# Two groups of second-stage products moved ahead of a mixing and of a transpose step, in a convolution and spectral mixing kernel

## The chip, the cores and the metric

The kernel runs on one core of one Trainium2 chip. The metric is the device time of one execution in microseconds (us): the median of several runs. A profiled execution gives, beside it, a trace of every instruction, and its span (the time from the first to the last recorded instruction).

## The reference

The input `x` has 8 sequences (B) of 3264 steps (S) with 192 channels (D). Two stages follow each other.

```python
# 1. a causal convolution over 7 steps, with softmax weights for each of 8 heads (24 channels each)
w = softmax(weight)                                  # (8 heads, 7 taps)
x = einsum('hk,bskhg->bshg', w, x_unf)               # x_unf: the last 7 steps, zero padded
# 2. a mixing of the 64 lowest Fourier modes, and a product with a matrix and a relu
X = rfft(x, axis=1)[:, :64]                          # Xr, Xi
Yr = einsum('bmd,mde->bme', Xr, w_r) - einsum('bmd,mde->bme', Xi, w_i)
Yi = einsum('bmd,mde->bme', Xr, w_i) + einsum('bmd,mde->bme', Xi, w_r)
y = irfft(Y, n=S, axis=1)                            # Y is zero above mode 64
u = x + y
return u + maximum(u @ w_ch, 0)
```

## The kernel before, in words

The order of the instructions on each engine is written out by hand (a manual schedule); each engine works through its own list in that order, and semaphores hold an instruction until what it needs is there. The two halves of a pair of sequences are always worked on together, so there are four pairs, q = 0 to 3.

**Convolution and transform (to about 71 us).** TensorE (PE) convolves tiles of 128 steps with a banded matrix (L297), VectorE (DVE) and ScalarE (ACT) copy the results to `xall`, and products with a table of sines and cosines (`ftab`, L358) give the Fourier modes of each pair.

**Mixing (to about 98 us).** The 64 modes are mixed in 16 groups of four: `mix(g, bank)` issues twelve small products (L515) with the weights of group g, which the DMA queue of GpSimd (POOL) brings in. There are eleven places for weights; a mixing asks, after its last product, for the weights of group g + 11, if there is such a group. Two groups share a PSUM bank, `zm[0]` or `zm[1]`. `mix_copy` (L525, L527, on ACT) scales the sums into `ymix`, and `mix_trans` transposes `ymix` by two or four products (L398) into the two banks `ze`, from which DVE (L552) and ACT (L554) copy them into `yet`. Between the steps of one mixing, `some(n)` puts other work, the transposes of `xall` into `ct` (L398, evicted at L393 and L395), as long as there is any.

**End of the mixing, where the change lies (about 98 to 105.5 us).** Groups 14 and 15 are mixed each by itself, and other work stands between their steps:

- `zw_pair(q, bw, by)` makes the second-stage products of a later pair, q = 1, 2 or 3. For both halves t of the rows (weights `wm` and `w1`) and both sequences of the pair, `zw_mm` issues two products (L591 and L592) of `yet` with the weights. The four of t = 0 write bank `bw`, the four of t = 1 bank `by`. ACT then copies `bw` (L602), DVE copies `by` (L604) into `zwl`. The products read all columns of `yet`, those of the last groups included; what they give for the last eight modes is overwritten later by `late_rows` (L533 to L539), which makes these rows anew and writes them by DMA.
- `both(n, first, "c")` issues the first pieces (six products, L582) of the output pair n of tiles, into the banks `place[n]`. `place[0]` is `sl[0:2]`; `place[1]` are the two banks that `ze` named until then, and from there on `ze` names `sl[2:4]`.
- At the end, four `zw_mm` make the second-stage products of pair 0, and three copies (L690, L691, L692) evict them into `zw`.

**Last stage (from 105.45 us).** For the 104 output tiles, PE adds the remaining products into a ring of eight banks (L716, L647), ACT applies the relu (L640), DVE adds `xall` (L629), and the queue of SyncE (SP) stores the result (L635).

Of the kernel before, what the change touches and what calls it, by code (L numbers as in the profile page):

```python
# [20 lines left out]
def kernel(  # L21
# [107 lines left out]
    def open_psum(side, widths):  # L129

        if side in stacks:
            stacks.pop(side).close()
        es = ExitStack()
        n = npool[0]
        npool[0] += 1
        p = es.enter_context(tc.tile_pool(name=f"ps{n}", bufs=1, space=PSUM, side=side, reuse_waits="tile"))
        stacks[side] = es
        return [p.tile([P, w, 512], F32, tag=f"z{n}_{i}", name=f"z{n}_{i}") for i, w in enumerate(widths)]
# [337 lines left out]
    ze, zm = [z[:, 0, :] for z in z4[0:2]], [z[:, 0, :] for z in z4[2:4]]  # L476
# [33 lines left out]
    def mix(g, bank):  # L510
        yp = bank[:, D * (g % 2):D * (g % 2) + D]
        for j in range(3):
            for p4 in range(4):
                m = 4 * g + p4
                nc.tensor.matmul(yp[32 * p4:32 * p4 + 2 * B, :], xt[:, j, :, m],  # L515
                                 wts[g][:, p4, j, :], start=(j == 0), stop=(j == 2),
                                 tile_position=(0, 32 * p4), skip_group_check=True)
        load_w(g + NW + NL)

    def mix_copy(d, bank, g0, n):  # L520

        g = 2 * d + g0
        srcv = bank[:, D * g0:D * (g0 + n)].rearrange("p (g d) -> p g d", g=n)
        if g == 0:
            nc.scalar.activation(out=ymix[:, 0, :], in_=srcv[:, 0, :], func=ACT.Copy, scale=ascale[:, 0:1])  # L525
            g, n, srcv = 1, n - 1, srcv[:, 1:n, :]
        nc.scalar.activation(out=ymix[:, g:g + n, :], in_=srcv, func=ACT.Copy, scale=2.0 / S)  # L527
# [14 lines left out]
    def mix_trans(d, g0, n):  # L542
        et = [z.bitcast(BF16)[:, 0:n * P].rearrange("p (g k) -> p g k", g=n) for z in ze]
        for t in range(2):
            for g in range(n):
                trans(et[t][:, g, :], ymix[:, 2 * d + g0 + g, 64 * t:64 * t + P])
        m0 = 8 * d + 4 * g0
        for t in range(2):
            dst = yet[:, t, 2 * B * m0:2 * B * (m0 + 4 * n)].rearrange("p (m k) -> p m k", k=2 * B)
            srcv = et[t].rearrange("p g (q k) -> p (g q) k", q=4)[:, :, 0:2 * B]  # L550
            if t == 0:
                nc.vector.tensor_copy(out=dst, in_=srcv)  # L552
            else:
                nc.scalar.copy(out=dst, in_=srcv)  # L554
# [14 lines left out]
    def both(n, first, which, begin=False, end=False):  # L569
        duo, banks = duos[n], place[n]  # L570
        lists = (z_pieces(duo[first], 0, which), z_pieces(duo[1 - first], 1, which))
        old = held.get(n)
        if old is not None and old[0] != first:
            turn(old[1])
        last = [None, None]
        for k in range(max(len(lists[0]), len(lists[1]))):
            for row in range(2):
                lst, bank = lists[row], first ^ row
                if k >= len(lst):
                    continue  # L580
                cols, l, r = lst[k]
                mm = nc.tensor.matmul(target(banks[bank], cols, r), l, r, start=(begin and k == 0),  # L582
                                      stop=(end and k == len(lst) - 1), skip_group_check=True)
                last[row] = mm.ins.name
        held[n] = (first, last)

    def zw_mm(b, o, t):

        cols = slice(D * t, D * t + D)
        last = 2 * MODES * B - B + b + 1  # L590
        nc.tensor.matmul(o, yet[:, 0, b:last:B], wm[:, cols], start=True, stop=False, skip_group_check=True)  # L591
        nc.tensor.matmul(o, yet[:, 1, b:last:B], w1[:, cols], start=False, stop=True, skip_group_check=True)  # L592

    def zw_pair(q, bw, by):

        for t, bank in enumerate((bw, by)):
            for i in range(2):
                zw_mm(2 * q + i, bank[:, D * i:D * i + D], t)
        for t, bank in enumerate((bw, by)):
            dst, srcv = zwl[:, 2 * q - 2:2 * q, t, :], bank[:, 0:2 * D].rearrange("p (b d) -> p b d", b=2)  # L600
            if t == 0:
                nc.scalar.copy(out=dst, in_=srcv)  # L602
            else:
                nc.vector.tensor_copy(out=dst, in_=srcv)  # L604
# [62 lines left out]
    sl = [z[:, 0, :] for z in open_psum("left", (1, 1, 1, 1))]  # L667
# [2 lines left out]
    mix_trans(d, 0, 2)  # L670
    both(0, 1, "c")
    zw_pair(1, ze[0], ze[1])
    d = ND - 1
    mix(NG - 2, zm[1])
    mix_copy(d, zm[1], 0, 1)
    zw_pair(2, sl[2], sl[3])
    mix_trans(d, 0, 1)
    zw_pair(3, zm[0], sl[2])
    mix(NG - 1, zm[1])
    mix_copy(d, zm[1], 1, 1)  # L680

# [127 lines left out]
```

## Time and profile before

| | |
|---|---|
| median of 3 runs | 173.54 us (173.25 to 173.95) |
| the profiled execution | 173.94 us, its span 172.2 us |
| granted clock of TensorE, mean | 0.988 |
| busy in the span | PE 160.6 (93%), weight loads 133.6 (78%), DVE 128.5 (75%), ACT 113.7 (66%), POOL 51.4 (30%) |
| 99.50 to 102.35 us | PE busy 2.21 of 2.85 us |
| 102.35 to 105.45 us | PE busy 3.01 of 3.10 us |
| weight loads (288 KB each) | about 11 us from issue to landing, the last issued at 90.85 us |
| output stores | 384 KB each, 3.8 us from issue to landing |

PE's matmuls are pipelined: a product of 192 columns shows some 250 ns, but products of one kind start about 80 ns apart, so distances between starts say more than durations. "PEld" are PE's weight loads, which run beside its products. In the chain of work, each step is followed back to what released it, and "issue" is time in which the engine waited for nothing that the profile shows. Profile lines name an instruction by its line of the kernel: L604 is DVE's copy of a second-stage bank, wherever `zw_pair` is called.

### The profile page before, as it was taken

Reading aid. Unit: us, or ns where it says so; the run is one execution under the profiler, and the core shown is the slowest. Engines: PE = TensorE matmul, PEld = TensorE weight load, DVE = VectorE, ACT = ScalarE, POOL = GpSimd, SP = SyncE. Lnnn points to the kernel's source line nnn. Section 1 sums busy time; section 2 is a strip of 40 time slices with the busy share of each in tenths; the row PEclk is TensorE's granted clock in tenths of the full one; section 3 lists DMA queues with packets and bytes.
Section 4 is the critical chain, followed back from the end, with each engine's and each line's share of the span. In section 5 each row is a group of like instructions: output and inputs, shape, how many; then the busy total and the mean of one; then the engine's idle time right before and its main releaser. Section 6 shows DMA issues by size and latency. Waiting matters only on the chain.

```text
span 172.2 us, 6925 instructions
## 1 busy us (share of the span) xinstructions
PE 160.6 (93%) x2897; PEld 133.6 (78%) x2897; DVE 128.5 (75%) x262; ACT 113.7 (66%) x226; POOL 51.4 (30%) x93
## 2 busy tenths in 40 slices
PE   6978999999998999979999989999999999999980
PEld 6974866877867777769999765799899898989840
DVE  4899964736737575567767736799998999999980
ACT  8485864545546366377777644688888888888860
POOL 7997522424323352444441000890000000000000
PEclk9999999999999999999999999999999999999995
DMA  2999999999999999999999940488999999989894
GB/s 31 202 203 203 207 201 203 204 204 202 205 202 205 208 205 207 206 206 206 209 203 206 209 69 4 161 298 321 361 334 350 348 320 339 351 318 358 299 386 170
DMA packets 37151, 40.14 MB, mean 233 GB/s; under 512 B 2464, under 2 KB 37120, under 8 KB 37120
## 3 DMA queue, kind: packets, MB, share of 16 engines
q0 software_dynamic: 22816, 19.62, 71.1%
q1 hardware_dynamic: 14304, 20.09, 31.9%
q8 instruction: 22, 0.36, 0.8%
q14 instruction: 9, 0.07, 0.1%
HBM read 39.10 MB, written 20.05 MB: 344 GB/s over the span
## 4 chain that ended last, share of the span: by engine, by line
PE 79%; DMA 10%; POOL 3%; ACT 2%; issue 1%; DVE 1%; POOLq 0%; ACTq 0%; DVEq 0%
PE z L716 34%; PE z L297 16%; PE z L398 12%; DMA xall<-in_x_dram 10%; PE z L358 10%; PE z L515 3%; POOL xall L153 3%; PE z L591 1%; PE z L647 1%; PE z L375 1%; PE z L592 1%; ACT ftab L393 1%; ACT z L479 1%; ACT shared L527 0%; PE z L582 0%
## 5 line engine op out<-in xcount | busy, mean ns | idle before, releaser
L629 DVE TENSOR_TENSOR arena<-z,xall 128x384 f32<-128x384 f32 (+1 forms) x103 | 56.4, 556 | 3.4 <-PE z L716 1.5
L640 ACT ACTIVATE z<-z 128x384 f32<-128x384 f32 x102 | 48.5, 475 | 12.2 <-PE z L716 2.4
L716 PEld LDWEIGHTS <-ct 64*128 64x128 bf16 x600 | 42.3, 94 | 3.7 <-PE z L647 0.6
L716 PE MATMUL z<-arena,ftab 64*128 64x384 bf16 x308 | 44.9, 322 | 0.0
L297 PE MATMUL z<-xall,shared 64*64 64x336 bf16 (+3 forms) x1024 | 39.0, 294 | 2.1 <-ACT shared L238 1.1
L297 PEld LDWEIGHTS <-shared 64*64 64x64 bf16 x1024 | 33.2, 106 | 8.1 <-issue 4.3
L716 PE MATMUL z<-wsw,ct 64*128 64x192 bf16 x300 | 35.1, 243 | 0.0
L344 DVE CAST xall<-z 128x336 bf16<-128x336 f32 (+1 forms) x48 | 22.9, 482 | 12.0 <-PE z L297 9.7
L716 PEld LDWEIGHTS <-ftab 64*128 64x128 bf16 x396 | 29.7, 93 | 2.7 <-issue 0.5
L342 ACT CAST xall<-z 128x336 bf16<-128x336 f32 (+1 forms) x48 | 20.1, 418 | 15.0 <-PE z L297 11.0
L716 PE MATMUL z<-wm,ct 64*128 64x192 bf16 x200 | 29.9, 243 | 0.0
L716 PE MATMUL z<-w,ct 64*128 64x192 bf16 x100 | 24.3, 243 | 0.0
L395 DVE COPY ct<-z 128x1024 bf16<-128x1024 bf16 x27 | 17.4, 685 | 5.5 <-PE z L398 2.4
L398 PE MATMUL z<-ident,xall 128*128 128x128 bf16 x312 | 19.8, 219 | 0.0
L358 PE MATMUL z<-xall,ftab 128*128 128x384 bf16 (+1 forms) x104 | 18.3, 327 | 0.8 <-DVE xall L336 0.8
L398 PEld LDWEIGHTS <-xall 128*128 128x128 bf16 x312 | 17.8, 98 | 1.0 <-issue 0.2
L153 POOL DMA_DIRECT2D xall<-in_x_dram x16 | 15.0, 944 | 10.3 <-DMA xall<-in_x_dram 9.3
L358 PEld LDWEIGHTS <-ftab 128*128 128x128 bf16 (+1 forms) x104 | 9.6, 98 | 8.1 <-issue 1.3
L716 PE MATMUL z<-mixa,ftab 64*128 64x384 bf16 x88 | 13.6, 323 | 0.0
L393 ACT COPY ct<-z 128x1024 bf16<-128x1024 bf16 x12 | 12.1, 1012 | 2.1 <-PE z L398 1.1
L539 POOL DMA_DIRECT2D arena<-xs x16 | 7.9, 504 | 16.9 <-ACT xs L535 16.9
L276 POOL DMA_DIRECT2D arena<-in_moe_w_r_dram x10 | 6.1, 615 | 9.9 <-ACT xall L342 4.7
(113 smaller groups left out, 154.3 us busy)
## 6 DMA issues: line engine op xcount, KB each, us to landing
out_dram<-arena SPq DMA_DIRECT2D x47, 384.0 KB, 3.8
xall<-in_x_dram POOLq DMA_DIRECT2D x8, 672.0 KB, 16.8
xall<-in_x_dram POOLq DMA_DIRECT2D x8, 480.0 KB, 16.8
arena<-in_moe_w_r_dram POOLq DMA_DIRECT2D x10, 288.0 KB, 11.0
arena<-in_moe_w_i_dram POOLq DMA_DIRECT2D x10, 288.0 KB, 11.3
ct<-in_moe_w_r_dram POOLq DMA_DIRECT2D x6, 288.0 KB, 11.4
ct<-in_moe_w_i_dram POOLq DMA_DIRECT2D x6, 288.0 KB, 11.4
out_dram<-arena SPq DMA_DIRECT2D x4, 288.0 KB, 3.5
```

The source lines that it names most:

```text
L153: nc.gpsimd.dma_start(out=xin[:, s0:s0 + nf, 2 * D * i:2 * D * (i + 1)], in_=src)
L297: yield nc.tensor.matmul(o, band[r, h, int(a != a1), c0:c0 + 64], xin5[r, s1:s1 + n, :, a1, dsl], start=(row == 0 and a1 == 0), stop=(row ...
L342: nc.scalar.copy(out=dst[:, a], in_=srcv)
L344: nc.vector.tensor_copy(out=dst[:, a], in_=srcv)
L358: nc.tensor.matmul(xp, ftab[0:k, t, :], xall[0:k, NT * q + t, :, :], start=(t == t0), stop=(t == t1 - 1), skip_group_check=True)
L393: nc.scalar.copy(out=out, in_=in_)
L395: nc.vector.tensor_copy(out=out, in_=in_)
L398: nc.tensor.matmul(o, in_, ident[:], start=True, stop=True, is_transpose=True)
L539: nc.gpsimd.dma_start(out=zwl[k:k + 1, :, :, :].rearrange("p b t d -> p b (t d)"), in_=ylate[r + 2:r + B, :])
L629: nc.vector.tensor_tensor(out=o[0:pn, :, a, :], in0=srcv, in1=xall[0:pn, s + a, :, :], op=ALU.add)
L640: nc.scalar.activation(out=z, in_=z, func=ACT.Relu)
L716: mm = nc.tensor.matmul(target(bank[k], cols, r), l, r, start=first, stop=last, skip_group_check=True)
```

## The change

Two calls of `zw_pair` move. That of pair 2 goes ahead of mixing 14 and its copy, right behind that of pair 1. That of pair 3 goes ahead of the transposes of mixing 14, which then stand right in front of mixing 15. Nothing else is changed, banks included.

```diff
     both(0, 1, "c")
     zw_pair(1, ze[0], ze[1])
+    zw_pair(2, sl[2], sl[3])
     d = ND - 1
     mix(NG - 2, zm[1])
     mix_copy(d, zm[1], 0, 1)
-    zw_pair(2, sl[2], sl[3])
+    zw_pair(3, zm[0], sl[2])
     mix_trans(d, 0, 1)
-    zw_pair(3, zm[0], sl[2])
     mix(NG - 1, zm[1])
     mix_copy(d, zm[1], 1, 1)
```

In the built program PE's list changes accordingly. On ACT, pair 2's copy (L602) goes ahead of mixing 14's (L527), and pair 3's ahead of the transposes' (L554). On DVE, pair 3's copy (L604) goes ahead of the transposes' (L552). The lists of POOL and SP stay the same. Pair 3's products lose their wait for L552 and L554; their fifth gains one for pair 2's L602, which evicts the bank that it writes. The first two L582 pieces of `both(1, 0, "c")` gain one each, for L552 and L554.

## The prediction

> **What bounds the kernel now.** First the page's chain of work that ended last:
>
> ```profile
> PE 79%; DMA 10%; POOL 3%; ACT 2%; issue 1%; DVE 1%; POOLq 0%; ACTq 0%; DVEq 0%
> ```
>
> TensorE (PE) carries the end for 79%, so a stall of PE is paid in full, if the last stage doesn't absorb it. The diff touches only the stretch between the first later pair's products and the last stage. There I read the chain in order of time, from 99 to 106 us (start, duration, what):
>
> ```profile
> 101.64 0.11 DVE arena L604
> 101.75 0.36 issue
> 102.11 0.19 DVE yet L552
> 102.31 0.05 issue
> 102.35 0.30 PE z L591
> ...
> 103.66 0.02 issue
> 103.68 0.34 ACT shared L527
> 104.02 0.05 issue
> 104.06 0.29 PE z L398 x2
> ```
>
> The chain leaves PE twice. At 101.64 it goes over VectorE (DVE): the eviction L604 of pair 2, then the copy L552 of the transposes into `yet`, which pair 3's products (L591/L592) wait for. At 103.68 it goes over ScalarE (ACT): the copy L527 of mixing 15, which the last transposes wait for. The waits of 98 to 112 us agree (engine, line, waited for: us, times, longest):
>
> ```profile
> PE z L591 <- DVE yet L552: 0.6, 1, 0.6
> PEld L398 <- ACT shared L527: 0.7, 2, 0.4
> ```
>
> DVE's own timeline shows why L552 is late: it stands behind L604.
>
> ```profile
> 100.49 0.56 DVE L604 CAST arena<-z 128x384 bf16<-128x384 f32 x1 [1.12 <-DMA arena<-in_moe_w_r_dram]
> 101.64 0.56 DVE L604 CAST arena<-z 128x384 bf16<-128x384 f32 x1 [0.59 <-PE z L592]
> 102.11 0.18 DVE L552 COPY yet<-z 128x64 bf16<-128x64 bf16 x1
> 103.34 0.56 DVE L604 CAST arena<-z 128x384 bf16<-128x384 f32 x1 [1.05 <-PE z L592]
> ```
>
> **The change, part by part.** Nothing is added or removed: 8 products, 12 mixing products, 2 transposes, 3 ACT and 2 DVE copies change places. None of the moved steps issues a DMA (mixings 14 and 15 ask for no further weights), and the queues of SP and POOL keep their order. Pair 3 no longer waits for `yet`, since the transposes that write it now come later. In exchange the first piece of output pair 1 (L582, into the banks that the transposes used) waits for L552 and L554; in the old order that was satisfied long before.
>
> Start-to-start steps of PE, from the timeline: product to product in a pair 0.08; a whole pair after a break, first to last start, 0.64 (100.72 to 101.36); a pair that follows a pair without a break 0.08 + 0.58; last product to a mixing 0.18 (100.15 to 100.33); mixing to what follows 0.39 (100.33 to 100.72); last product to transposes 0.08; transposes to what follows 0.22 (104.06 to 104.28); six L582 pieces to what follows 0.36 (104.28 to 104.64).
>
> Before, from pair 1's last product at 100.15: 0.18 + 0.39 + 0.64 + 0.08 + 0.22 + 0.64 + 0.18 + 0.39 = 2.72 gives 102.87 for the first L582; it stands at 103.55, so the wait inside is 0.68. The transposes after it could start at 103.55 + 0.36 = 103.91 and start at 104.06: 0.15 more. After, without waits: 0.08 + 0.58 + 0.18 + 0.39 + 0.64 + 0.08 + 0.22 + 0.39 = 2.56: 0.16 less, since one break between kinds of work is gone.
>
> Now the new order in time. Pair 2's products start at 100.23 to 100.81, mixing 14 at 100.99, pair 3 at 101.38 to 102.02, transposes at 102.10, mixing 15 at 102.32, L582 at 102.71 if nothing holds it. What could hold each:
> - Pair 3's fifth product (101.77) needs bank `sl[2]`, from which ACT's L602 evicts pair 2. L602 starts 0.28 to 0.29 after the fourth product (three rows): 100.48 + 0.29 = 100.77, plus 0.48: 101.25. Cover 0.52. Without that cover, each later ns of L602 goes into the end.
> - The transposes (102.10) need mixing 14's L527: 0.51 after the mixing's start, 0.33 long: 101.83. Covered by pair 3, by 0.27.
> - Mixing 15 (102.32) needs its weights; the loads below.
> - L582 needs L552, which now stands behind pair 3's L604. L604 starts 0.28 to 0.35 after the last product (three rows); I take 0.35, as in the two where DVE had been idle: 102.37 to 102.93. L552 started 0.09 before its predecessor's end (102.11 against 102.20), so 102.84, takes 0.18 to 103.02, and PE went on 0.06 later (102.29 to 102.35): 103.08. **New wait: 0.37.** L554, behind ACT's L602 of pair 3 (to 102.45), ends at 102.67 and isn't last.
> - The last transposes could start at 103.08 + 0.36 = 103.44; mixing 15's L527 (102.32 + 0.52 + 0.33, and 0.06 until PE goes on) lets them go at 103.23. That old wait is gone.
>
> So the transposes stand at 103.44 instead of 104.06. From there the order is the old one, and the timeline of 105 us and later names PE, the new copies or a bank as releaser, no load: all of it shifts. **Sum: 0.68 + 0.15 + 0.16 - 0.37 = 0.62 us.** Bounds: with no new wait, L582 at 102.71 and the transposes held by L527 until 103.23, 0.83; with neither, 0.99; and 0 if mixing 15 can't start earlier than it did.
>
> The row on DVE: L552 began 0.09 before L604 ended. [...]
>
> Row on the loads (stretch, busy times by engine, granted clock, DMA share, GB/s):
>
> ```profile
> 101.25:101.50 0.25, 0.25 (x7) 0.25 (x5) 0.00 (x0) 0.19 (x1) 0.00 (x0) 1.00 0.41 69
> 101.50:101.75 0.25, 0.21 (x4) 0.04 (x1) 0.11 (x1) 0.25 (x1) 0.00 (x0) 1.00 0.08 9
> 101.75:102.00 0.25, 0.00 (x0) 0.00 (x0) 0.25 (x1) 0.23 (x2) 0.00 (x0) 1.00 0.00 0
> ```
>
> The last load is issued at 90.85, and the loads of these lines land 10.9 to 11.2 after issue: by 102.05, against 102.32 wanted. A landing later by up to 0.27 costs nothing, nor do 0.21 more, by which L527 (103.23) precedes what the transposes wait for (103.44).
>
> The profiled execution took 173.94 (span 172.2 and 1.74 around it), so 173.32 by its own sum; it stands 0.40 above the median 173.54, from which 0.62 leads to 172.9.
>
> **The rivals.**
> 1. *The new wait isn't there.* If pair 3's L604 or L552 comes earlier (the third L604 row started 0.28 after its last product, not 0.35), or L582's first pieces get by, the gain is 0.83 to 0.99: 172.55 to 172.7. For it: PE has other work until 102.71, and only one short copy is in the way. Against: DVE is strictly in order in every view, and L604's 0.56 is the same in all rows.
> 2. *The load of mixing 15 becomes the wait.* It decides from a landing after 102.5 on; at 103.16, where mixing 15 started before, the gain is nil: 173.5. Against: 102.05 in this trace, and no traffic after 101.75. [...]
> 3. *Slower: VectorE becomes the bound of the stretch.* Its three L604 now stand in a row ahead of L552, on which L582 waits. With d for one, back to back from 100.49, the transposes come at 100.49 + 3d - 0.09 + 0.18 + 0.06 + 0.36 = 101.00 + 3d: no gain from d = 1.02, over 0.5% slower from d = 1.31; at 1.5 they come 1.44 late: 175.0. For it: ACT's evictions and the loads' writes to the same buffer fall closer together. Against: d was 0.56 both at a DMA share of 0.45 and at none, beside ACT and alone.
> 4. *The last stage absorbs the gain.* From 120 on DVE is busy 18.93 and 19.47 of 20 us and waits for PE alone, nothing there waits for an output transfer: it starts earlier and ends earlier. That the order isn't what the diff says is excluded by the built program's lists. I fold both into the second rival's chance.
>
> **How the numbers follow.** Forecast 0.52 (gain 0.45 to 0.85), first rival 0.29, second with the fourth 0.08, third 0.11. The bound of 0.5%, 0.87 us, is about what a measurement of this kernel can tell from no change; the three runs before spread over 0.70. A third of the forecast's chance (0.18) lies beyond it, with the spread of medians and the terms' ends, and most of the first rival's (0.23): faster 0.41. Slower is the third rival: 0.11. Within: 0.48. The likeliest case's own range is 172.65 to 173.1. The range 172.4 to 173.6 takes in the first rival with 0.15 of spread below it, and no gain above; it leaves out the third rival and some 0.08 below.
>
> **What would show it.** Right: pair 3's first product about 1.0 us earlier, its L591 no longer waiting for L552; L582 waiting for L552 by 0.3 to 0.45; L398 no longer waiting for mixing 15's L527; the first L716 at about 104.8 instead of 105.45, the last stage as long as before. Wrong: L591 waiting for ACT at pair 3's fifth product; mixing 15 waiting for a load; L604 rows above 0.6; or a last stage that is longer by what was won.

## The result, and the profile after

The changed kernel takes 173.00 us (median of 20 runs, 172.55 to 173.53) against 173.69 for the kernel before in the same draw, a set of runs taken together (20 runs, 173.04 to 174.41): a ratio of 0.9961, 95% interval 0.9951 to 0.9972, that is 0.68 us less, 0.49 to 0.85. The prediction had 0.62 less, and within 0.5% as the likeliest outcome.

The chain of work after, in order of time around the place where pair 3 waited before (start, duration, what):

```profile
102.54 0.08 PE z L592
102.62 0.11 PE z L398 x2
102.73 0.42 PE z L515 x12
103.15 0.05 issue
103.20 0.19 DVE yet L552
103.39 0.04 issue
103.43 0.42 PE z L582 x6
```

In this stretch the chain now leaves PE once instead of twice, and later: pair 3's products, the transposes and mixing 15 follow each other without a gap, then the first L582 waits for L552. The step over ACT's L527 of mixing 15 is gone. In the waits of 98 to 112 us, the line of L591 that waited 0.6 us for L552 is gone, and these stand there:

```profile
PEld L398 <- ACT shared L527: 0.4, 1, 0.4
PE z L582 <- DVE yet L552: 0.3, 1, 0.3
```

The one wait left for L527 is that of the mixing before (at 99.19), which the change doesn't touch. DVE's timeline shows the new order, pair 1's and pair 2's evictions merged in the first line, pair 3's ahead of L552:

```profile
100.85 1.16 DVE L604 CAST arena<-z 128x384 bf16<-128x384 f32 x2 [1.11 <-DMA arena<-in_moe_w_i_dram]
102.72 0.56 DVE L604 CAST arena<-z 128x384 bf16<-128x384 f32 x1 [0.71 <-PE z L398]
103.20 0.18 DVE L552 COPY yet<-z 128x64 bf16<-128x64 bf16 x1
```

The span is 171.5 us instead of 172.2, but two spans don't show where the time went. Pair 1's first product began at 99.52 in the trace before and at 99.88 in this one: what lies ahead of it differs between executions. So does what lies behind: from the start of PE's last product to the end of the span it is 5.40 us before and 5.01 after, and two executions of one kernel (pair 3 alone moved, below) have 5.38 and 5.15. So I read **the stretch**, from pair 1's first product (L591) to the first L716: 105.45 - 99.52 = 5.93 before, 105.18 - 99.88 = 5.30 after, 0.63 less. From the first L716 to the start of PE's last product it takes 61.32 us in both.

### The profile page after: what moved, and what is told of

Its sections match the earlier page's. It is cut to its first block, busy times and chain, and to the rows that moved or that the text cites. A ratio compares the mean times of both kernels' runs of the same rounds, so it can differ in the third digit from the quotient of the medians.

```text
span 171.5 us, 6925 instructions
## 1 busy us (share of the span) xinstructions
PE 161.1 (94%) x2897; PEld 134.8 (79%) x2897; DVE 128.3 (75%) x262; ACT 113.7 (66%) x226; POOL 51.8 (30%) x93
## 4 chain that ended last, share of the span: by engine, by line
PE 80%; DMA 10%; POOL 3%; ACT 2%; issue 1%; DVE 0%; POOLq 0%; ACTq 0%; DVEq 0%
PE z L716 34%; PE z L297 16%; PE z L398 12%; DMA xall<-in_x_dram 10%; PE z L358 10%; PE z L515 3%; POOL xall L153 3%; PE z L647 1%; PE z L591 1%; PE z L375 1%; PE z L592 1%; PE z L582 1%; ACT ftab L393 1%; ACT z L479 1%; POOL xall L157 0%
## 5 line engine op out<-in xcount | busy, mean ns | idle before, releaser
L716 PEld LDWEIGHTS <-ct 64*128 64x128 bf16 x600 | 42.3, 94 | 3.7 <-PE z L647 0.6
L716 PE MATMUL z<-arena,ftab 64*128 64x384 bf16 x308 | 44.9, 322 | 0.0
L716 PE MATMUL z<-wsw,ct 64*128 64x192 bf16 x300 | 35.1, 243 | 0.0
L716 PEld LDWEIGHTS <-ftab 64*128 64x128 bf16 x396 | 29.7, 93 | 2.7 <-issue 0.5
L716 PE MATMUL z<-wm,ct 64*128 64x192 bf16 x200 | 29.9, 243 | 0.0
L716 PE MATMUL z<-w,ct 64*128 64x192 bf16 x100 | 24.3, 243 | 0.0
L716 PE MATMUL z<-mixa,ftab 64*128 64x384 bf16 x88 | 13.6, 323 | 0.0
L184 PE MATMUL z<-xall 128*128 128x144 bf16 x85 | 7.9, 276 | 1.6 <-DVE xall L171 1.6
```

What stands on the lines that cost most here:

```text
L184: nc.tensor.matmul(free[3][:, 0, 0:144], zeros[:, 0:P], zeros[:, 0:144], start=True, stop=True, skip_group_check=True)
L716: mm = nc.tensor.matmul(target(bank[k], cols, r), l, r, start=first, stop=last, skip_group_check=True)
```

## The experiments

Theory A is the prediction's: pair 3's wait for `yet` is replaced by a shorter one behind VectorE's eviction, and each us of the stretch reaches the end. Its rivals: B, what pays is that pair 2's eviction is out of L552's way; C, the time doesn't hang on the stretch but on what lies behind PE's last product; and the prediction's second rival, the load of mixing 15. The table has all kernels; ratios are to the kernel before in the same draw.

| kernel | stretch, us | time, ratio (95%) | in us |
|---|---|---|---|
| before | 5.93 | 1 | |
| the change | 5.30 | 0.9961 (0.9951 to 0.9972) | -0.68 |
| pair 2 alone moved | 6.06 | 1.0003 (0.9988 to 1.0017) | +0.05 |
| pair 3 alone moved | 5.36 | 0.9982 (0.9968 to 0.9995) | -0.31 |
| the same, second draw | 5.36 | 0.9967 (0.9955 to 0.9979) | -0.57 |
| before, pair 2's eviction behind L552 | 5.60 | 0.9995 (0.9984 to 1.0005) | -0.09 |
| the same, second draw | 5.61 | 0.9989 (0.9978 to 1.0001) | -0.19 |
| the change, pair 3's eviction behind L552 | 5.14 | 0.9956 (0.9943 to 0.9968) | -0.76 |
| the same, mixing 15 without its load | 5.06 | 0.9950 (0.9933 to 0.9966) | -0.87 |
| the change, mixing 15 without its load | 5.29 | 0.9960 (0.9942 to 0.9978) | -0.69 |
| the change, pair 3's eviction twice | 5.89 | 0.9990 (0.9968 to 1.0011) | -0.17 |
| the change, pair 3's eviction five times | 7.66 | see below | |
| the change, pair 3's eviction twelve times | 13.01 | 1.0502 (1.0445 to 1.0559) | +8.7 |

In all of them but the last, PE's last product comes 61.32 us after the first L716. The stretch is from one profiled execution each. The table speaks against C: each kernel whose stretch is shorter by 0.5 us or more is faster with an interval clear of 1, and those whose stretch is within 0.14 us of the old one (pair 2 alone, the eviction twice) are not; the two draws with 0.32 lie in between.

**Pair 2 alone moved.**

```diff
     zw_pair(1, ze[0], ze[1])
+    zw_pair(2, sl[2], sl[3])
     d = ND - 1
     mix(NG - 2, zm[1])
     mix_copy(d, zm[1], 0, 1)
-    zw_pair(2, sl[2], sl[3])
     mix_trans(d, 0, 1)
     zw_pair(3, zm[0], sl[2])
```

> Only pair 2's products go ahead of mixing 14; pair 3 stays behind the transposes, so it still waits for the copy into yet. The stretch is read from pair 1's first product to the first L716: 5.93 us before, 5.30 after the change. Theory A (pair 3's wait for yet is what the change removes): nothing is gained. The transposes now stand right behind mixing 14 and wait for its L527, until about 1.89 + 100.0 on the clock of the trace before, L552 comes 0.27 after them, and pair 3 starts at about 102.40 instead of 102.35: stretch 5.9 to 6.0, ratio to the kernel before 0.999 to 1.001. Theory B (what pays is that pair 2's eviction L604 is out of L552's way on VectorE): about 0.4 of the 0.63 us comes with this move alone, stretch about 5.5, ratio about 0.998. Theory C (the stretch is not what the time hangs on; the shorter end of the span after the last product is): no run of this set differs from the kernel before by its stretch.

Nothing is gained; the stretch is 0.14 longer. The chain of this kernel shows that the old wait stays and a new one comes ahead of it:

```profile
100.80 0.41 PE z L515 x12
101.21 0.02 issue
101.23 0.34 ACT shared L527
101.57 0.05 issue
101.62 0.30 PE z L398 x2
...
101.98 0.20 DVE yet L552
102.19 0.05 issue
102.23 0.30 PE z L591
```

Without pair 2 between them, the transposes wait for mixing 14's L527; then pair 3 waits for L552, though no eviction stands ahead of that on DVE any more. B is wrong: with this move alone, L552 out of the eviction's way is worth nothing, since the transposes ahead of it have lost their cover. What is over the 5.9 to 6.0 expected is L552's: it starts 0.36 after the first transpose (101.62 to 101.98), where 0.27 had been taken, from the last transposes (104.06 to 104.33 in the trace before).

**Pair 3 alone moved.**

```diff
     zw_pair(2, sl[2], sl[3])
-    mix_trans(d, 0, 1)
     zw_pair(3, zm[0], sl[2])
+    mix_trans(d, 0, 1)
     mix(NG - 1, zm[1])
```

> Only pair 3's products go ahead of the transposes; pair 2 stays behind mixing 14. Theory A: nearly the whole gain. Pair 3's fifth product waits some 0.07 us for ScalarE's eviction of pair 2, the copy L552 again stands behind pair 3's L604, and the first L582 waits for it: stretch 5.38 (0.55 less than before), ratio about 0.997. Theory B: at most 0.2 us of gain, stretch 5.7 or more. Theory C: no relation between stretch and time.

The stretch is 5.36, 0.57 of the 0.63, as A has it. What is missing is the wait that the text above expects of pair 3's fifth product, for ACT's eviction of pair 2 out of the same bank:

```profile
101.28 0.48 ACT L602 CAST arena<-z 128x384 bf16<-128x384 f32 x1
101.81 0.24 PE L591 MATMUL z<-wm,yet 128*128 128x192 bf16 x1
```

The product ahead of it started at 101.66; without a wait the step is 0.08, here it is 0.15. The time was 0.31 less, with an interval (0.09 to 0.56) that just misses 0.57. So this kernel and the one of the next experiment, which missed likewise, were run in a second draw.

> The kernel with pair 3 alone moved, once more on another draw of runs. Its stretch was 0.57 us shorter than before, its time 0.31 (0.09 to 0.56). Theory A (every us of the stretch reaches the end, and the first ratio is low by chance): the stretch is 5.36 again and the two draws together lie round a ratio of 0.9967. Theory E (a part of this gain is lost elsewhere): a ratio of 0.998 again, and a last stage over 61.32 us or a later start of the stretch.

The second draw gives the stretch again and 0.57 less time, with the last stage at 61.32 as before, so nothing shows a loss elsewhere; the smaller gain of the first draw was probably chance.

**The old order, pair 2's eviction behind L552.** TensorE's list is that of the kernel before. For this run and the others that move or repeat an eviction, `zw_pair` has two more arguments: which evictions to issue (0 is ScalarE's, 1 is VectorE's), and whether to make the products; the diffs show the calls alone.

```diff
-    zw_pair(2, sl[2], sl[3])
+    zw_pair(2, sl[2], sl[3], (0,))
     mix_trans(d, 0, 1)
+    zw_pair(2, sl[2], sl[3], (1,), False)
     zw_pair(3, zm[0], sl[2])
```

> The old order of TensorE, but pair 2's VectorE eviction (L604) is issued behind L552. Theory A: of the wait of 0.68 the part in which L552 stands behind L604 goes: L552 starts 0.27 after the transposes, at 101.71 instead of 102.11, pair 3 starts 0.40 earlier, the wait for L527 stays: stretch 5.53, ratio about 0.998. If pair 3 waits for something else (a bank, a load): stretch 5.93, no difference.

> The old order with pair 2's eviction behind L552, once more. Its stretch was 0.32 us shorter than before, its time 0.09 (0.28 shorter to 0.09 longer). Theory A: the stretch is 5.60 again, and the ratio lies round 0.998. Theory E: round 0.9995 again.

The stretch is 0.32 shorter (0.40 expected; the rest again the 0.36 from transposes to L552). The profile puts that L552 down to ACT's L602, which ends within 0.01 us of its start, here and in the next kernel; but the same 0.36 passes in the kernel with pair 2 alone moved, where L602 was over long before, so I don't count it as the cause. So of the 0.68 of waiting before, about half was the eviction ahead of L552, and the other half the way from the transposes through the copy to PE, which only other work can cover. The time is 0.19 less in the second draw (0.38 less to 0.02 more), which holds 0.32; the first draw (0.28 less to 0.09 more) just misses it. Between the two, the size of the gain in time isn't settled better than that.

**The changed kernel, pair 3's eviction behind L552.**

```diff
-    zw_pair(3, zm[0], sl[2])
+    zw_pair(3, zm[0], sl[2], (0,))
     mix_trans(d, 0, 1)
+    zw_pair(3, zm[0], sl[2], (1,), False)
     mix(NG - 1, zm[1])
```

> The changed kernel, with pair 3's VectorE eviction (L604) issued behind the copy L552 of the transposes instead of ahead of it; nothing else moves. Theory A: the new wait goes. L582 starts 0.36 earlier, at the end of mixing 15; then the last transposes are held by mixing 15's L527, so 0.23 of it arrives: stretch 5.07, ratio to the kernel before about 0.995, and about 0.2 us faster than the changed kernel. Theory B expects the same of this one. A theory in which L582 waits for mixing 15 or the loads anyway: stretch 5.30 as in the changed kernel.

The new wait is gone, and the stretch is 5.14, some 0.15 less than with the change. Two waits are left. The timeline shows both, the load that mixing 15 waits for and L527 ahead of the last transposes:

```profile
102.00 0.28 PE L398 MATMUL z<-ident,shared 128*128 128x128 bf16 x2
102.29 0.26 PEld L515 LDWEIGHTS <-mixa 128*16 128x16 bf16 x12 [0.19 <-DMA arena<-in_moe_w_i_dram]
102.36 0.19 DVE L552 COPY yet<-z 128x64 bf16<-128x64 bf16 x1 [0.80 <-ACT arena L602]
...
102.69 0.26 PE L582 MATMUL z<-wm,ct 64*128 64x192 bf16 x2
...
103.18 0.11 PEld L398 LDWEIGHTS <-shared 128*128 128x128 bf16 x2 [0.30 <-ACT shared L527]
```

Of the kernels that leave nothing out it has the shortest stretch; against the change the times (0.9956 and 0.9961, from two draws) don't tell them apart.

**The same, mixing 15 without its load.** Modes 60 to 63 are made from the weights of group 14.

```diff
-                                 wts[g][:, p4, j, :], start=(j == 0), stop=(j == 2),
+                                 wts[min(g, NG - 2)][:, p4, j, :], start=(j == 0), stop=(j == 2),
```

> The changed kernel with pair 3's VectorE eviction behind L552, and mixing 15 made from the weights of group 14 (modes 60 to 63 come out of other weights). With the eviction behind L552 alone, mixing 15 started 2.86 us after pair 1's first product instead of 2.78, and the page named a load as the releaser. Theory A: that 0.08 is the last load's landing; here mixing 15 starts at 2.78 and the stretch is 5.07 instead of 5.14. If the 0.08 has another cause (the transposes' slower end, say): 5.14 again.

Mixing 15 starts at 2.78 and the stretch is 5.06, as expected. But this run by itself doesn't show that the load made the 0.08: its pair 1 began at 99.73, so mixing 15 was due at 102.51, when the load (landed at 102.28 by the trace's semaphore records) would have been there anyway. What shows it is the trace of the kernel above: there pair 1 began early (99.43), mixing 15 was due at 102.21, the load landed at 102.25, and mixing 15 started at 102.29. This is the prediction's second rival, met in one execution once the new wait is gone.

**The changed kernel, mixing 15 without its load.** The same edit of the weights, in the changed kernel itself.

> The changed kernel, with mixing 15 made from the weights of group 14 (modes 60 to 63 come out of other weights), so that it waits for no late load; the loads themselves stay. Theory A: no load is late in the changed kernel, stretch 5.30 and the time unchanged, ratio to the kernel before 0.996. If the landing of the last load holds mixing 15 or what follows: the stretch becomes shorter, by up to 0.2 us.

No difference: no load is seen to be late in the changed kernel. Its own trace says the same: the load landed at 102.02, and mixing 15 started at 102.66. The cover hangs on when pair 1 begins, though: in the trace with the eviction twice (next), which has the same order up to there, it was 0.09 (102.22 to 102.31).

**The eviction issued several times.** The same copy (L604) of the same data again, ahead of L552, once, four or eleven times more.

```diff
     zw_pair(3, zm[0], sl[2])
+    for _ in range(n): zw_pair(3, zm[0], sl[2], (1,), False)      # n = 1, 4 or 11
     mix_trans(d, 0, 1)
```

> The changed kernel, with pair 3's VectorE eviction issued twice (the same copy a second time), ahead of L552: a known delay of 0.56 us on the link that the prediction names as the new wait. Theory A: L552 and so L582 and everything behind come 0.56 later: stretch 5.86, and the time is 0.56 us over the changed kernel's, ratio to the kernel before about 0.9995. If the copy isn't the last to arrive, or if the last stage absorbs a later start: less than that, down to 0 (ratio 0.996).

```profile
102.40 0.55 DVE arena L604
102.95 0.02 issue
102.97 0.04 DVE arena L604
103.01 0.44 issue
103.45 0.19 DVE yet L552
103.64 0.04 issue
103.68 0.42 PE z L582 x6
```

The chain goes through the evictions, L552 and the first L582. One copy more costs 0.60 of the stretch (0.56 of the copy and 0.04 until the next one starts), and the time rises from 0.68 below to 0.17 below.

> The changed kernel with pair 3's VectorE eviction issued five times ahead of L552 (four copies more, 0.596 us each by the run with one more): a delay of 2.38 us on the same link. Theory A (the copy is the link, and every us of the stretch reaches the end): stretch 5.30 + 2.38 = 7.68, the time 2.38 over the changed kernel's, ratio to the kernel before about 1.010, and the last stage 61.32 us as in all other runs. If the last stage takes up a part of a later start: it is shorter than 61.32 and the ratio below 1.008.

The profiled execution does what A says: stretch 7.66, last stage 61.32, 175.3 us. Of the six executions two took 175.3 and 175.4, the others 177.0, 177.6, 179.8 and 180.1 (over the four shorter ones the ratio is 1.0162, 1.0117 to 1.0206): a part of them met something more. The mean granted clock of each execution is on record: 0.997 and 0.996 in the two shortest, 0.988 and 0.989 in the next two, 0.964 and 0.963 in the two longest, where all executions of the kernels with fewer copies lie between 0.988 and 1.000. So in the two longest the clock was low for some time more than in any of those; the two at 177 us lie at the edge, and there the mean doesn't tell, since a fall behind PE's last product alone (0.50 from 168.2 us to the end) gave 0.988 in the trace before. That it was the stall that lowered the clock these numbers don't show, so a longer stall was made to show it in a trace.

> With five evictions in a row the profiled execution took 175.3 us, as the stretch says, but four of its six executions took 177.0 to 180.1. This kernel makes the stall long enough to show in a profile what they meet: twelve evictions in a row ahead of L552 (eleven copies more, 6.56 us), so that TensorE idles some 6.9 us. Theory A, the delay alone: 6.56 over the changed kernel, 179.6, and a granted clock of 1.0 behind the stall. Theory D (the stall closes TensorE's clock gate): the granted clock falls below 1.0 within or behind the stall for some microseconds, the work in them takes up to twice as long, and the time is 1.7 to 4.5 us more than that, 181 to 184, with a last stage of more than 61.32 us.

Theory D holds: within the stall the granted clock falls to 0.50, and the work behind it runs slower: the second-stage products there start 0.16 us apart (L592 at 111.40, L591 at 111.56), against 0.08 in the other traces. The windows of this kernel (stretch, busy us of PE, PEld, DVE, ACT and POOL, granted clock, DMA share, GB/s):

```profile
98.00:102.50 4.50, 4.31 (x74) 3.37 (x66) 2.25 (x6) 2.64 (x7) 0.00 (x0) 1.00 0.68 115
102.50:106.00 3.50, 0.18 (x12) 0.09 (x1) 3.29 (x7) 0.43 (x2) 0.00 (x0) 0.83 0.00 0
106.00:109.50 3.50, 0.00 (x0) 0.00 (x0) 3.28 (x7) 0.00 (x0) 0.00 (x0) 0.50 0.00 0
116.50:118.00 1.50, 1.50 (x11) 0.56 (x10) 0.93 (x2) 0.00 (x0) 1.35 (x3) 0.50 0.02 3
118.00:120.00 2.00, 2.00 (x29) 1.20 (x29) 1.11 (x3) 0.98 (x3) 2.00 (x5) 0.88 0.64 206
```

PE is idle from 102.68 (0.18 us into the second window) to 109.5. The clock is full until it falls to 0.50: the mean of 0.83 puts that 0.17 * 3.5 / 0.5 = 1.2 us ahead of 106.0, at 104.8. It stays there until 118.5 (0.88 over the last window), 9 us of them with PE at work. That costs 13.01 - (5.30 + 6.56) = 1.15 us in the stretch and 63.92 - 61.32 = 2.60 in the last stage; the median is 183.1 (mean clock 0.958 to 0.977 in its four executions), where the delay alone would have given 179.8 in this draw (173.91 - 0.68 + 6.56).

## Why the prediction was right, point by point

**What bounds the kernel.** That a stall of PE here is paid in full held: the last stage takes 61.32 us in ten kernels whose stretch lies between 5.06 and 7.66. The fourth rival, that the last stage takes the gain up, is wrong.

**The terms.** Counted from pair 1's first product (99.52 in the trace that the prediction used, 99.88 in the one after), pair 3 was forecast at 1.86, mixing 15 at 2.80, the first L582 at 3.56 and the last transposes at 3.92; they stand at 1.86, 2.78, 3.55 and 3.91. The new wait of 0.37 is 103.43 - (102.66 + 0.39) = 0.38. The sum of 0.62 measures 0.63 in the stretch and 0.68 (0.49 to 0.85) in time.

**The covers** held too: pair 3's fifth product (102.12) came well after ACT's L602 had ended (101.60), and the transposes (102.45) after mixing 14's L527 (102.18). The clock times that the prediction gave as signs (the first L716 at 104.8) were off, at 105.18, as pair 1 began 0.36 later in this execution; distances from a common start would have been the better sign.

**Which move pays.** The prediction gave one sum for both. The runs share it out: pair 3's move gives 0.57, pair 2's alone loses 0.14, and on top of pair 3's it gives 0.06: pair 2's eviction on ACT is then over before pair 3's fifth product needs the bank, which waits 0.07 for it otherwise. The break between kinds of work that the sum counts as gone (0.16) is gone by either move alone.

**DVE's order.** The eviction ahead of L552 is the link, as the runs with more copies and with the copy behind show. The overlap that the prediction took from the trace before (0.09) is there again, at 0.08: L552 starts at 103.20, while the eviction ahead of it is recorded until 103.28. One number of this link was in part luck: the 0.35 from pair 3's last product to L604 came out (102.37 to 102.72), but the reason given for taking it over 0.28 doesn't, as DVE had been idle ahead of all three rows (0.59 ahead of the one with 0.28).

**The rivals.** The first, no new wait, didn't come by itself; made by hand, it gives 5.06 without the load's wait, 0.87 less than before and inside the 0.83 to 0.99 given for it. The second, the load, is not there in the change and is there, with 0.08 in one trace, one step further. The third, VectorE as the bound, has its slope right (0.60 us per copy), but its evictions took 0.56 as before. It had a limit that it didn't name: with 2.7 us of idle PE, four of six executions took 1.7 to 4.7 us more than the delay.

## What to carry to other kernels

When an engine waits for a result that it doesn't need, moving its work ahead of the producer takes that wait away, but look what the moved work puts ahead of the copy that others need: here an eviction of 0.56 us ahead of a copy of 0.18 made a new wait of 0.38. With the eviction behind the copy the stretch was some 0.15 shorter, and some 0.24 where no load was late; the rest went to the next wait. Lay the new order out with start-to-start steps from the trace, counted from one common start, and check each wait in the built program; here that gave every station within 0.02 us. And once a wait is gone, ask which one is next: here a load and a ScalarE copy stood right behind it.

## What the runs showed of the hardware

A stall of PE cost more than its length in two of these kernels. With up to 0.9 us of idle in one piece of the stretch (all kernels up to two evictions) the last stage took 61.32 us, and the mean granted clock of every execution was 0.988 to 1.000; in the traces before and after it stayed at 1.00 until PE's last product had ended. With 2.7 us (five evictions) the profiled execution kept 1.00 through the stall and the work behind it (102 to 116 us), and four of six took 1.7 to 4.7 us more, the two longest at a mean clock of 0.964 and 0.963. With 6.8 us it fell to half 2.1 us after the last product ahead of the stall and stayed there for 13.7 us, 4.7 of them in the stall; 9 us of work passed before the clock rose again.

The length of the idle time alone doesn't decide it, as 2.7 us of it left the clock up in one trace and 2.1 us brought it down in the other. Behind PE's last product the same shows: the clock fell to 0.50 some 1.1 us after that product's end in the trace before (167.09 to 168.16) and some 3.7 us after it in the trace after (166.82 to 170.5). What decides it, and why executions of one kernel differ, as the six with five evictions did, no run here shows.
